# q and k in three tiles of 17, 17 and 16 chunks instead of five of 10, with eight output buffers and six held groups

## The chip, the cores and the metric

The kernel runs on one core of a Trainium2 chip. The core has a matrix engine (PE, with its weight loads shown as PEld), a vector engine (DVE), a scalar engine (ACT), a general engine (POOL), a queue engine (SP) and 16 DMA engines that move data between HBM and the on-chip memory. The metric is the time of one execution in microseconds; lower is better.

## The reference

Two stages. Per batch (B = 4, N = 6400 rows, C = 256 columns) an attention across channels, and then a mixture of eight low-rank adapters on every row of its result, of which each row takes two:

```python
qn = q / (norm(q, axis=1) + 1e-6);  kn = k / (norm(k, axis=1) + 1e-6)     # over the 6400 rows
s  = kn.T @ qn / tau                                                      # 256 x 256 per batch
a  = softmax(s, axis=-1)
x  = v @ a                                                                # 6400 x 256 per batch
logits = x @ w_gate                                                       # 8 experts
w  = softmax over the two largest logits of a row
out = x + sum over those two e of  w_e * (x @ A[e]) @ B[e]                # rank 16
```

So all of a batch's q and k must be read before the first output row of that batch can be made, while v is used row by row. Inputs and outputs are fp32 in HBM.

## The kernel before

**Chunks.** A batch's 6400 rows are 50 chunks of 128 rows; partition p holds rows 50p to 50p + 49, so a load of n chunks reads n KB in one piece per partition. Loads of q, k and v are issued on POOL and turn fp32 into bf16 on the way: a 10-chunk row becomes 5 KB. q and k share one tile (`qk`, both halves, `PC` = 10 chunks, `QKB` = 4 buffers). v comes in tiles of 18, 16 and 16 chunks (`VP`, three buffers); for batch 0 each of these is loaded in two pieces, all but 8 chunks and then 8. The v of the last batch (20, 20, 10 chunks) uses the q/k ring, which is free by then. One tile (`SPLIT`) is loaded in several row pieces.

**Per chunk.** `gram` (L265) adds k^T q of one chunk to a PSUM bank with two matmuls (L271). `square` (L253) squares q and k of two chunks at once on ACT (L261) or, for every second pair of batch 0, on DVE (L263); `norm` (L276) sums the squares on PE. After the 50th chunk, `chain0` to `chain6` make the softmax and fold it into two matrices: `a` for y and `wa` for logits and rank-16 products. `chain2` (L327) multiplies a scaled copy of the gram (`tk`) by a broadcast factor into `s_sb` (L331 to L334).

**Per pair of chunks** (100 pairs, called units u): four PE transposes of v (`transposes`, L421) with a copy to SBUF; after every five units a group is complete, its `logits` and `gating` follow (with one exponential on ACT, L490); then `z_gz` (L527), `gz_t`, `y_mm` (L543) and `delta` (L563), which copies the result into the group's output buffer on ACT (L567).

**Order.** All is written out by hand. First batch 0: squares, grams and norms of its 50 chunks. Then 100 slots: slot s transposes unit s, and carries the grams of the next batch that the table `GRAM` deals it (batch 1 in slots 0 to 20, batch 2 in 24 to 45, batch 3 in 49 to 67), while z and y of earlier units follow some groups behind. Squares of a slot stand at its start, so ACT and DVE meet them in that order.

**Loads.** A list sorted by the slot that needs each load is issued in order by `load_more` (L144): a load whose buffer is still in use stops all behind it. Each DMA on POOL also waits for the one issued eight places before it. Before the identity matrices are made on POOL, four q/k tiles of batch 0 are asked for (`load_more(3)`, `load_more(1)`); the first 4 chunks come by SP.

**Stores.** An output group is a 1.31 MB buffer, `YB` = 9 of them, the first of which serves as staging at the start. `send` (L577) issues stores on ACT's queue: it holds back `DEFER` = 7 complete groups while loads are left to issue, and one fewer for every three slots after the last load is issued. The last ten units are stored in small pieces on SP (L571).

Of the kernel before, what the change touches and what calls it, by code (L numbers as in the profile page):

```python
# [8 lines left out]
FP32 = mybir.dt.float32  # L9
BF16 = mybir.dt.bfloat16  # L10
AX = mybir.AxisListType
OP = mybir.AluOpType
ACT = mybir.ActivationFunctionType
# [3 lines left out]
def kernel(  # L17
# [16 lines left out]
    nc = tc.nc  # L34
    B, N, C = q.shape
    P = 128
    NC = N // P
    CC = C // P
# [3 lines left out]
    assert ER == P and CC == 2 and N % P == 0  # L42
    inv_tau = 1.0 / float(tau)

    PC = 10
    NPAIR = NC // 2
    NPT = B * NPAIR
    GRP = 5
    QKB, VB, YB = 4, 3, 9

    VP = [[18, 16, 16]] * 3 + [[20, 20, 10]]
    SPLIT = (1, 2)
    ROWS, ROWS_C = (7, 34, 6, 68, 13), 2
    FIRST = 4
    DEFER = 7

    GRAM = {1: (0, 20), 2: (24, 45), 3: (49, 67)}
    assert B == 4 and NC == 50
# [13 lines left out]
    one = ctx.enter_context(tc.tile_pool(name="one", bufs=1))  # L72
# [13 lines left out]
    qk_need = {}  # L86
    for b, (first, last) in GRAM.items():
        n = last - first + 1
        for c in range(NC):
            s = first + c * n // NC  # L90
            todo.setdefault(s, []).append((b, c))
            qk_need.setdefault((b, c // PC), s)


    loads = []

    for s in range(NC // PC):
        o = FIRST if s == 0 else 0
        loads.append((-10 + s, "qk", 0, s, o, [6, 4] if s == NC // PC - 1 else [PC - o]))
        for b in range(1, B):  # L100
            loads.append((qk_need[b, s], "qk", b, s, 0, [PC]))
    for b in range(B):
        for s, n in enumerate(VP[b]):
            at = NPAIR * b + sum(VP[b][:s]) // 2 + 1
            if b == 0:
# [6 lines left out]
    tiles = {"qk": {}, "v": {}}  # L112
    left = {"qk": [], "v": []}
# [4 lines left out]
    def ring(kind, b):  # L118
        return "qk" if b == B - 1 else kind

    def piece(kind, b, c):

        if kind == "qk":
            return divmod(c, PC)
        s = 0
        while c >= VP[b][s]:
            c -= VP[b][s]
            s += 1
# [5 lines left out]
    def load_by_rows(dst, src, m):  # L134

        dst = dst.rearrange("p (g c) d -> p g c d", g=2)
        src = src.rearrange("p (g c) d -> p g c d", g=2)
        nc.gpsimd.dma_start(dst[:, :, ROWS_C:m // 2, :], src[:, :, ROWS_C:m // 2, :])
        r = 0
        for n in ROWS:  # L140
            nc.gpsimd.dma_start(dst[r:r + n, :, 0:ROWS_C, :], src[r:r + n, :, 0:ROWS_C, :])
            r += n

    def load_more(limit=1000):  # L144

        while limit and at_load[0] < len(loads):
            _, kind, b, s, o, parts = loads[at_load[0]]
            if (kind, b, s) not in where:
                r = ring(kind, b)
                n = len(left[r])  # L150
                if n >= bufs[r] and left[r][n - bufs[r]]:
                    return
                where[kind, b, s] = n
                left[r].append(PC if kind == "qk" else VP[b][s])
                if r == "qk":
                    t = qk_pool.tile([P, 2, PC, C], BF16, tag="qk", name="qk")
                    if kind == "v":
                        t = t.rearrange("p w c d -> p (w c) d")
                else:
                    t = v_pool.tile([P, max(VP[b]), C], BF16, tag="v", name="vt")  # L160
                tiles[kind][b, s] = t
            t = tiles[kind][b, s]
            c0 = s * PC if kind == "qk" else sum(VP[b][:s])
            for m in parts:
                if kind == "qk":
                    nc.gpsimd.dma_start(t[:, 0, o:o + m, :], q_v[b, :, c0 + o:c0 + o + m, :])  # L166
                    nc.gpsimd.dma_start(t[:, 1, o:o + m, :], k_v[b, :, c0 + o:c0 + o + m, :])
                elif (b, s) == SPLIT:
                    load_by_rows(t[:, o:o + m, :], v_v[b, :, c0 + o:c0 + o + m, :], m)
                else:  # L170
                    nc.gpsimd.dma_start(t[:, o:o + m, :], v_v[b, :, c0 + o:c0 + o + m, :])
                o += m
            at_load[0] += 1
            limit -= 1
# [13 lines left out]
    DL = E * C // P  # L188
    nc.sync.dma_start(ast, moe_A.rearrange("e (h l) r -> (e h) (l r)", l=DL))
    load_more(3)  # L190
    ones_bf = const.tile([P, P], BF16)
    nc.vector.memset(ones_bf, 1.0)
# [4 lines left out]
    for c in range(0, FIRST, 2):  # L197
        t = tiles["qk"][0, 0]
        nc.vector.tensor_copy(t[:, 0, c:c + 2, :], stage[:, 0, c:c + 2, :])
        nc.scalar.copy(t[:, 1, c:c + 2, :], stage[:, 1, c:c + 2, :])  # L200
    load_more(1)
    ident = const.tile([P, P], BF16)
    make_identity(nc, ident)
    ident_f = const.tile([P, P], FP32)
    make_identity(nc, ident_f)
    load_more(3)

    wg_sb = const.tile([P, CC, E], BF16)
# [43 lines left out]

    def square(b, c, eng):  # L253

        s, o = divmod(c, PC)
        t = tiles["qk"][b, s]
        sq = sq_pool.tile([P, 2, 2, C], BF16, tag="sq", name="sq")
        sqs[b, c] = sq
        src = t[:, :, o:o + 2, :]
        if eng == "act":  # L260
            nc.scalar.activation(sq, src, ACT.Square)  # L261
        else:
            nc.vector.tensor_tensor(out=sq, in0=src, in1=src, op=OP.mult)  # L263

    def gram(b, c):  # L265
        if c == 0:
# [60 lines left out]
    def chain2(b):  # L327
        d = st[b]
        bc = nrm[b][:, 256:512]
        nc.tensor.matmul(bc, ones_f, d["dg"].rearrange("p c d -> p (c d)"), start=True, stop=True)  # L330
        s_sb = one.tile([P, CC, C], FP32, name="s_sb")  # L331
        for ic in range(CC):
            nc.vector.tensor_tensor(out=s_sb[:, ic, :], in0=bc, in1=d["tk"][:, ic, :], op=OP.mult)
        d["s"] = s_sb  # L334

    def chain3(b):
# [44 lines left out]
    def chain6(b):  # L381
        d = st[b]
        a_bf = bat.tile([P, CC, C], BF16, name="a_bf")
        for ic in range(CC):
# [3 lines left out]


    CHAIN = [(chain0, 0.0), (chain1, 0.9), (chain2, 0.75), (chain3, 0.0), (chain4, 0.55),  # L390
             (chain5, 0.65), (chain6, 0.5)]

# [184 lines left out]
    def send(keep):  # L577


        eng = nc.scalar  # L580
        while len(unsent) > keep:
            gr = unsent.pop(0)
            c0, n = 2 * (gr["f"] - gr["b"] * NPAIR), 2 * gr["n"]
            eng.dma_start(out_v[gr["b"], :, c0:c0 + n, :], gr["ys"][:, 0:n, :])
# [4 lines left out]
    for c in range(0, NC, 2):  # L589
        square(0, c, "act" if (c // 2) % 2 else "dve")  # L590
        gram(0, c)
        gram(0, c + 1)
        load_more()

        if c == 12:
            mask, sel = spread_masks()
        elif c in (20, 24, 28, 32):
            spread_rows(c - 20, 4)
        elif c == 36:
            cast_constants()  # L600
            spread()
        if c >= 4:
            norm(0, c - 4)
            norm(0, c - 3)
# [31 lines left out]
    while nz < NPT or zq is not None or dq is not None:  # L636
# [7 lines left out]
        for b, c in items:  # L644
            if c % 2 == 0:
                square(b, c, "act")
        if f in (chain0, chain1, chain2, chain3):
            f(fb)
# [15 lines left out]
        if at_load[0] < len(loads):  # L664
            all_loads[0] = slot
        send(max(0, DEFER - (slot - all_loads[0]) // 3))
        if behind:
# [53 lines left out]
```

## Time and profile before

| | |
|---|---|
| time, median of 3 runs (lowest, highest) | 255.47 us (255.2, 255.64) |
| the profiled execution's own time | 255.28 us |
| its span in the trace | 253.5 us |
| PE, DVE, ACT, POOL busy | 222.4, 155.5, 176.5, 35.4 us |
| granted PE clock, mean | 0.964 |
| HBM read, written | 78.91 MB, 26.21 MB: 415 GB/s over the span |

Times in the trace are counted from the span's start. A row of the timeline gives start, duration, engine, line, operation, output and input, and in brackets the idle time before it with what ended it; "q" behind an engine's name means its queue processor, which issues DMAs. In the chain a row is start, length and what held the end up. In a table by stretches a row gives a stretch, its length, the busy time of each engine with the number of instructions, the granted PE clock, the share of the DMA engines and GB/s. Rows of DMA issues give output and input, queue, count, KB each (as written) and the time from issue to landing.

### The profile page before, as it was taken

How to read it: one execution, taken by the hardware profiler on the slowest of the kernel's cores; microseconds unless marked ns; L12 is line 12 of the kernel's file. 1: busy time of each engine (PE TensorE's matmuls, PEld its weight loads, DVE VectorE, ACT ScalarE, POOL GpSimd, SP SyncE). 2: the span in 40 equal slices, each digit the busy share in tenths (PEclk: the TensorE clock that was granted, in tenths of full speed). 3: DMA queues.
4: the chain of work that ended last, by engine and by line, in shares of the span. 5: the costliest groups of instructions: out<-in, count | busy, mean ns of one | idle time of the engine just before them, and what ended most of it. 6: DMA issues, size and time to landing. Idle time of an engine off the chain costs nothing.

```text
span 253.5 us, 7433 instructions
## 1 busy us (share of the span) xinstructions
PE 222.4 (88%) x3122; PEld 191.8 (76%) x3122; DVE 155.5 (61%) x583; ACT 176.5 (70%) x291; POOL 35.4 (14%) x70
## 2 busy tenths in 40 slices
PE   0769793895999999999999989999998899999991
PEld 0436471684899978989999878989997689999980
DVE  1325534355477677785876867667588487777760
ACT  2434353867388788877888787888865967778881
POOL 8031221112111010512140202000000000000000
PEclk9988999598699999999999999999999999999999
DMA  7999999999999999999999999999999999999996
GB/s 211 230 213 217 208 218 212 213 218 213 213 212 215 220 210 216 219 211 214 201 216 215 211 253 278 221 309 267 271 267 282 294 363 427 426 422 424 423 413 274
DMA packets 13953, 66.81 MB, mean 264 GB/s; under 512 B 2528, under 2 KB 3040, under 8 KB 10720
## 3 DMA queue, kind: packets, MB, share of 16 engines
q0 software_dynamic: 9600, 38.80, 75.4%
q10 hardware_dynamic: 2592, 23.59, 22.4%
q1 hardware_dynamic: 1728, 3.94, 4.3%
q8 instruction: 24, 0.39, 0.6%
q14 instruction: 9, 0.07, 0.1%
HBM read 78.91 MB, written 26.21 MB: 415 GB/s over the span
## 4 chain that ended last, share of the span: by engine, by line
PE 56%; DMA 28%; DVE 8%; ACT 3%; issue 3%; POOL 1%; DVEq 0%; ACTq 0%; POOLq 0%
PE y_ps L543 14%; DMA qk<-in_k_dram 13%; DMA vt<-in_v_dram 9%; PE acc L271 9%; PE zg L527 7%; PE y_ps L563 7%; PE vT_ps L421 6%; DMA out_dram<-ys 6%; PE zg L551 4%; PE nrm L288 3%; PE vT_ps L442 3%; ACT sq L261 2%; DVE gz L531 2%; ACT ys L567 1%; DVE lm L477 1%
## 5 line engine op out<-in xcount | busy, mean ns | idle before, releaser
L261 ACT ACTIVATE sq<-qk 128x1024 bf16<-128x1024 bf16 x87 | 89.6, 1054 | 18.6 <-DMA qk<-in_k_dram 12.3
L271 PE MATMUL acc<-qk 128*128 128x256 bf16 x400 | 75.1, 289 | 13.8 <-DMA qk<-in_k_dram 7.3
L567 ACT COPY ys<-y_ps 128x512 f32<-128x512 f32 x100 | 58.7, 587 | 24.8 <-PE y_ps L563 20.4
L543 PE MATMUL y_ps<-a_bf,vT 128*128 128x256 bf16 x400 | 60.3, 273 | 1.5 <-ACT ys L567 1.5
L271 PEld LDWEIGHTS <-qk 128*128 128x128 bf16 x400 | 34.7, 102 | 24.0 <-DMA qk<-in_k_dram 9.3
L531 DVE TENSOR_TENSOR gz<-zg,gate 128x256 bf16<-128x256 f32 x100 | 41.6, 417 | 14.3 <-PE zg L527 12.8
L432 DVE COPY vT<-vT_ps 128x512 bf16<-128x512 bf16 x63 | 26.7, 423 | 28.0 <-PE vT_ps L421 27.3
L288 PEld LDWEIGHTS <-sq 128*128 128x128 bf16 x600 | 36.4, 98 | 7.0 <-ACT sq L261 2.8
L527 PE MATMUL zg<-wa_sb,vT 128*128 128x128 bf16 x400 | 38.7, 220 | 1.2 <-DVE gzT L557 1.0
L563 PE MATMUL y_ps<-ball_sb,gzT 128*128 128x256 bf16 x200 | 38.5, 274 | 0.0
L288 PE MATMUL nrm<-ones_bf,sq 128*128 128x1 bf16 x600 | 35.9, 165 | 1.2 <-ACT sq L261 1.2
L543 PEld LDWEIGHTS <-vT 128*128 128x128 bf16 x400 | 33.6, 97 | 4.4 <-issue 1.6
L421 PE MATMUL vT_ps<-ident,vt 128*128 128x128 bf16 x300 | 30.1, 225 | 1.4 <-DMA vt<-in_v_dram 1.1
L430 ACT COPY vT<-vT_ps 128x512 bf16<-128x512 bf16 x37 | 21.7, 586 | 10.6 <-PE vT_ps L421 9.2
L551 PE MATMUL zg<-ident,gz 128*128 128x128 bf16 x200 | 27.9, 221 | 1.1 <-DVE gz L531 0.6
L527 PEld LDWEIGHTS <-vT 128*128 128x128 bf16 x400 | 26.1, 97 | 3.3 <-issue 2.1
L421 PEld LDWEIGHTS <-vt 128*128 128x128 bf16 x300 | 22.7, 100 | 3.6 <-DMA vt<-in_v_dram 1.3
L557 DVE COPY gzT<-zg 128x256 bf16<-128x256 bf16 x90 | 25.2, 280 | 0.0
L166 POOL DMA_DIRECT2D qk<-in_q_dram x21 | 11.5, 549 | 77.5 <-ACT sq L261 23.0
L263 DVE TENSOR_TENSOR sq<-qk 128x1024 bf16<-128x1024 bf16 x13 | 9.1, 701 | 19.6 <-DMA qk<-in_k_dram 11.1
L551 PEld LDWEIGHTS <-gz 128*128 128x128 bf16 x200 | 15.3, 98 | 2.9 <-DVE gz L531 2.5
L563 PEld LDWEIGHTS <-gzT 128*128 128x128 bf16 x200 | 16.1, 98 | 0.4
(73 smaller groups left out, 202.3 us busy)
## 6 DMA issues: line engine op xcount, KB each, us to landing
out_dram<-ys ACTq DMA_DIRECT2D x18, 1280.0 KB, 17.3
qk<-in_q_dram POOLq DMA_DIRECT2D x18, 640.0 KB, 18.9
qk<-in_k_dram POOLq DMA_DIRECT2D x18, 640.0 KB, 22.4
vt<-in_v_dram POOLq DMA_DIRECT2D x3, 1024.0 KB, 28.2
vt<-in_v_dram POOLq DMA_DIRECT2D x5, 512.0 KB, 22.4
qk<-in_v_dram POOLq DMA_DIRECT2D x2, 1280.0 KB, 30.5
vt<-in_v_dram POOLq DMA_DIRECT2D x2, 1152.0 KB, 18.4
out_dram<-ys SPq DMA_DIRECT2D x3, 512.0 KB, 6.2
```

The lines of the kernel that those rows point to most:

```text
L261: nc.scalar.activation(sq, src, ACT.Square)
L271: nc.tensor.matmul(acc[b][:, ic, :], t[:, 1, o, ic * P:(ic + 1) * P], t[:, 0, o, :], start=(c == 0 and ic == 0), stop=(c == NC - 1), skip_ ...
L288: nc.tensor.matmul(nrm[b][:, j:j + 1], sq[:, w, c % 2, ic * P:(ic + 1) * P], ones_bf[:, 0:1], start=(c == 0 and j == 0), stop=(c == NC - 1 ...
L421: nc.tensor.matmul(pt[:, ic, sc * P:(sc + 1) * P], vt[:, o + sc, ic * P:(ic + 1) * P], ident, is_transpose=True, start=(i == 0), stop=(i = ...
L432: nc.vector.tensor_copy(dst, src)
L527: nc.tensor.matmul(z[:, sc, :], r["vT"][:, ic, sc, :], st[b]["wa"][:, ic, E:E + ER], start=(sc == 0 and ic == 0), stop=(sc == 1 and ic == ...
L531: nc.vector.tensor_tensor(out=gz.rearrange("p c (e r) -> p c e r", e=E), in0=z.rearrange("p c (e r) -> p c e r", e=E), in1=gr["gate"][:, r ...
L543: nc.tensor.matmul(y[:, sc, :], r["vT"][:, ic, sc, :], st[b]["a"][:, ic, :], start=(sc == 0 and ic == 0), stop=False, skip_group_check=True)
L551: nc.tensor.matmul(gt[:, sc, :], r["gz"][:, sc, :], ident, is_transpose=True, start=(sc == 0), stop=(sc == 1))
L557: nc.vector.tensor_copy(gzT, gt)
L563: nc.tensor.matmul(r["y"][:, sc, :], r["gzT"][:, sc, :], ball_sb, start=False, stop=(sc == 1), skip_group_check=True)
L567: nc.scalar.copy(gr["ys"][:, r["w"]:r["w"] + 2, :], r["y"])
```

## The change

q and k of a batch are cut into tiles of 17, 17 and 16 chunks (`QKP`) with three buffers, so 51 chunks of room in place of 40. Batch 0's tiles are loaded in pieces of 6 and 7 (behind the 4 from SP), 9 and 8, and 8, 4 and 4 chunks; other batches' tiles in one piece. A pair of chunks can now lie across two tiles (chunks 16 and 17), and is then squared in two instructions. The last batch's v is cut into 34 and 16 chunks. There are eight output buffers and six held groups. `chain2` writes its product over `tk` in place of a buffer of its own.

```diff
-    PC = 10
+    PC = 17
+    QKP = [17, 17, 16]
...
-    QKB, VB, YB = 4, 3, 9
+    QKB, VB, YB = 3, 3, 8
 
-    VP = [[18, 16, 16]] * 3 + [[20, 20, 10]]
+    VP = [[18, 16, 16]] * 3 + [[34, 16]]
...
-    DEFER = 7
+    DEFER = 6
...
-    for s in range(NC // PC):
+    for s, n in enumerate(QKP):
         o = FIRST if s == 0 else 0
-        loads.append((-10 + s, "qk", 0, s, o, [6, 4] if s == NC // PC - 1 else [PC - o]))
+        loads.append((-10 + s, "qk", 0, s, o, [[6, 7], [9, 8], [8, 4, 4]][s]))
         for b in range(1, B):
-            loads.append((qk_need[b, s], "qk", b, s, 0, [PC]))
+            loads.append((qk_need[b, s], "qk", b, s, 0, [n]))
...
-                left[r].append(PC if kind == "qk" else VP[b][s])
+                left[r].append(QKP[s] if kind == "qk" else VP[b][s])
...
     def square(b, c, eng):
...
+        if o < PC - 1:
+            parts = [(sq, tiles["qk"][b, s][:, :, o:o + 2, :])]
         else:
+            parts = [(sq[:, :, 0, :], tiles["qk"][b, s][:, :, o, :]),
+                     (sq[:, :, 1, :], tiles["qk"][b, s + 1][:, :, 0, :])]
+        for dst, src in parts:
+            if eng == "act":
+                nc.scalar.activation(dst, src, ACT.Square)
+            else:
+                nc.vector.tensor_tensor(out=dst, in0=src, in1=src, op=OP.mult)
...
-        s_sb = one.tile([P, CC, C], FP32, name="s_sb")
+        s_sb = d["tk"]
         for ic in range(CC):
-            nc.vector.tensor_tensor(out=s_sb[:, ic, :], in0=bc, in1=d["tk"][:, ic, :], op=OP.mult)
+            nc.vector.tensor_tensor(out=s_sb[:, ic, :], in0=bc, in1=s_sb[:, ic, :], op=OP.mult)
```

More of the change, by code (lines that the diff above doesn't have):

```diff
@@ L253, in square @@
     def square(b, c, eng):
-        s, o = divmod(c, PC)
-        t = tiles["qk"][b, s]
         sq = sq_pool.tile([P, 2, 2, C], BF16, tag="sq", name="sq")
         sqs[b, c] = sq
-        src = t[:, :, o:o + 2, :]
-        if eng == "act":
-            nc.scalar.activation(sq, src, ACT.Square)
-        else:
-            nc.vector.tensor_tensor(out=sq, in0=src, in1=src, op=OP.mult)
+        s, o = divmod(c, PC)
+        if o < PC - 1:
+            parts = [(sq, tiles["qk"][b, s][:, :, o:o + 2, :])]
+        else:
+            parts = [(sq[:, :, 0, :], tiles["qk"][b, s][:, :, o, :]),
[5 more added lines that the diff above has]
+                nc.vector.tensor_tensor(out=dst, in0=src, in1=src, op=OP.mult)
     def gram(b, c):
```

## The prediction

> **What bounds the kernel now.** I read the page first (slices, queues), then the chain, then the stretches around the places where the chain is a transfer.
>
> ```profile
> span 253.5 us, 7433 instructions
> ...
> PE   0769793895999999999999989999998899999991
> ...
> PEclk9988999598699999999999999999999999999999
> DMA  7999999999999999999999999999999999999996
> ...
> q0 software_dynamic: 9600, 38.80, 75.4%
> q10 hardware_dynamic: 2592, 23.59, 22.4%
> ```
>
> The DMA engines are full nearly all the time, and PE too from slice 10 on. The chain tells which of the two decides where:
>
> ```profile
> 16.80 19.07 DMA qk<-in_k_dram
> ...
> 39.21 23.02 DMA vt<-in_v_dram
> 62.28 0.61 PE vT_ps L421 x4
> ...
> 182.13 14.24 DMA out_dram<-ys
> 196.44 0.59 ACT ys L567
> ...
> 248.01 0.59 ACT ys L567
> ```
>
> Up to 62.3 us the arrival of data decides. Batch 0's last k piece lands at 35.87 and the third v piece at 62.23; slot 9's transposes start on it at 62.28. From there it is compute, with one more transfer, a store that lands at 196.4.
>
> ```profile
> core 0: us, PE busy (x) PEld busy (x) DVE busy (x) ACT busy (x) POOL busy (x), PEclk, DMA share, GB/s
> 57.50:60.00 2.50, 0.48 (x9) 0.29 (x6) 1.34 (x6) 0.79 (x2) 0.07 (x1) 1.00 1.04 210
> 63.00:66.00 3.00, 3.00 (x31) 2.44 (x30) 0.97 (x3) 0.78 (x1) 0.74 (x2) 0.50 1.05 215
> 66.00:69.00 3.00, 3.00 (x48) 2.69 (x47) 1.90 (x8) 1.54 (x2) 0.18 (x2) 0.62 1.02 206
> 73.00:77.00 4.00, 4.00 (x65) 3.74 (x63) 2.26 (x7) 3.06 (x5) 0.53 (x1) 1.00 1.05 213
> L421 PE MATMUL vT_ps<-ident,vt x56: 215/219/315, 47.2 to 73.2; 128*128 128x128 bf16 x56
> 73.08 0.39 PE L421 MATMUL vT_ps<-ident,vt 128*128 128x128 bf16 x4
> ```
>
> Around 73 to 77 us PE is busy 4.00 of 4.00 us at full clock: time lost ahead of that point has nothing to be won back from. The last two rows place slot 13: 56 transposes are 14 slots, and the fourteenth set starts at 73.08.
>
> **Order of the loads (the main term).** The rate: between 35.87 and 62.23 land 60 chunks of q and k of batch 1 and 26 of v, 86 chunks in 26.36 us, 0.3065 us each. In the changed program the loads after batch 0 stand as: 34 chunks (q and k, 0 to 16), v 10, v 8, 34 (17 to 33), v 8, 32 (34 to 49), v 8 (chunks 26 to 33), v 8, v 8. A q/k tile is now 34 chunks in front of the v piece behind it, where it was 20. Landings by that rate from 35.87, with the slot that needs them:
> - first v, 44 chunks: 49.4 (slot 0; it was 30 chunks, 45.1).
> - second q/k tile, 86 chunks: 62.2. Its first chunk, 17, is used in slot 7.
> - third v, 94: 64.7 (slot 9; was 62.2).
> - third q/k tile, 126: 74.5 (slot 14).
> - fourth v, 134: 76.9 (slot 13; was 114 chunks, 70.8).
>
> ```profile
> 47.20 0.63 PE L421 MATMUL vT_ps<-ident,vt 128*128 128x128 bf16 x4
> 56.23 0.38 PE L271 MATMUL acc<-qk 128*128 128x256 bf16 x2
> 48.39 0.53 POOL L171 DMA_DIRECT2D vt<-in_v_dram  x1 [2.51 <-DMA qk<-in_q_dram]
> vt<-in_v_dram POOLq DMA_DIRECT2D x1, 512.0 KB, 22.4
> ```
>
> The last two rows check the rate: that v piece was issued at 48.39 and took 22.4, so 70.8. It was no wait then, since slot 13 came at 73.08. It becomes one: slot 13 cannot start before 77.0, 3.9 us late. The other way to the same place: slot 7's first gram (56.23 now) waits for 62.2, and the six slots from there took 73.08 - 56.23 = 16.9 us, 2.0 of them idle (the stretch from 57.50 above, 0.48 busy of 2.50), so 62.2 + 14.9 = 77.1. Both give 77. Behind the same wait stands ACT: the square of chunks 16 and 17 is issued in slot 6, its second half waits for chunk 17, and behind it in ACT's queue are the first group's exponential (so its gates) and the squares from 18 on. They have until 77 and need eight squares of 1.05 us, so they cost nothing beside PE's own wait. From slot 13 on I keep +3.9; later tiles land 2 to 10 us ahead of their slots by the same count, so nothing gives it back or adds.
>
> **Start.** All 14 loads of batch 0 now stand ahead of the identity matrices on POOL, and each waits for the one eight places before it. The last waits for the sixth, 52 of batch 0's 100 chunks (8 of them by SP): 35.87 - 48 x 0.3065 = 21.2, so the matrices come at 21 to 23 in place of 5.67:
>
> ```profile
> 5.67 0.24 POOL masks.py:197 MEMSET ident<- 128x128 bf16 x1
> 21.73 0.60 PE L271 MATMUL acc<-qk 128*128 128x256 bf16 x4
> 22.65 0.61 PE L271 MATMUL acc<-qk 128*128 128x256 bf16 x4
> ```
>
> DVE's masks at chunk 12 wait for them, behind them its squares, behind those PE's norms: PE stands at about 24.5 where data were there at 21.2. Bounds 0 to +2 at the end of batch 0; when data are there PE takes 0.92 us per two chunks (22.65 - 21.73) against 4 x 0.3065 = 1.23 of transfer and has 14 us to catch up, so I take 0. The cover is slot 0's wait for v until 49.4, 2.2 us after 47.20, and then slot 7's.
>
> **Stores.** Eight output buffers and six held groups: group 12's first copy now needs group 4's store landed, where it needed group 3's; either is issued after 55 copies. So the distance is the same and what counts is how long the store takes beside the loads.
>
> ```profile
> out_dram<-ys ACTq DMA_DIRECT2D x1, 1280.0 KB, 10.9
> out_dram<-ys ACTq DMA_DIRECT2D x1, 1280.0 KB, 14.2
> 182.13 0.34 ACTq L584 DMA_DIRECT2D out_dram<-ys  x1
> 196.44 0.58 ACT L567 COPY ys<-y_ps 128x512 f32<-128x512 f32 x1 [2.87 <-DMA out_dram<-ys]
> 155.20 0.56 POOL L171 DMA_DIRECT2D vt<-in_v_dram  x1
> DMA to landing us min/median/max: 29.6/29.6/29.6
> ```
>
> From the queues' shares: q0's 75.4% of 16 x 253.5 us over 38.80 MB is 0.079 us per KB written, q10's 22.4% over 23.59 MB 0.0385. A store's row (10 KB) takes 0.39 us, a load's row of 10 chunks (5 KB) 0.40, of 20 chunks 0.81, of 34 chunks (17 KB) 1.37. The first store (146.6, beside 10-chunk rows) took 10.9 us, that of 182.13 (beside 20-chunk rows) 14.2. With 8 rows per engine, taken in turn with load rows: 10.9 = a + 8 x 0.79 gives a = 4.6, and 4.6 + 8 x 1.20 = 14.2, as measured. So a load's long row holds the store up.
> In the changed kernel the 34-chunk load of v starts when the v piece before it is in, 184.8 now (155.20 + 29.6), plus most of one more store sent by then (1.31 MB, 3.1 us): about 187. It needs 34 x 0.3065 = 10.4 us alone and 13.4 in turn with store rows, to 200. Group 4's store goes out at 182.13 + 3.9 = 186.0, its rows from about 189.5: six beside 34-chunk rows (6 x 1.76), two beside 16-chunk ones (2 x 1.03), and 1.1 at the end: it lands near 203. The copy is ready at 196.44 - 2.87 + 3.9 = 197.5 and waits 5.5 us, 2.6 more than now. Bounds: -2.9 (no wait) to +5.5 (all eight rows beside 34-chunk ones and both wait and load later). I take +2.6, by the row of 182.13, the nearest.
>
> **The rest.**
> ```profile
> L261 ACT ACTIVATE sq<-qk 128x1024 bf16<-128x1024 bf16 x87 | 89.6, 1054 | 18.6 <-DMA qk<-in_k_dram 12.3
> L430 ACT COPY vT<-vT_ps 128x512 bf16<-128x512 bf16 x37 | 21.7, 586 | 10.6 <-PE vT_ps L421 9.2
> out_dram<-ys SPq DMA_DIRECT2D x2, 256.0 KB, 3.9
> stage<-in_q_dram SPq DMA_DIRECT2D x1, 512.0 KB, 3.9
> ```
> Squares: one per batch is halved; a half on ACT lies between 0.53 and 1.05, by the 128x512 copy 0.59, so 2 x 0.59 - 1.05 = +0.1 each; +0.2 for those beside a full PE. The product in place in chain2 has the same 8 instructions, its buffer's last reader is a batch earlier: 0. PE's sequence is unchanged. End: the last stores took 3.9 us behind others; a 512 KB load with nothing ahead also took 3.9, of which half its bytes are 0.6, so with compute later and the queue empty 3.3: -0.6.
> Sum, on the profiled execution's 255.28 (0.19 below the median 255.47): 255.28 + 3.9 + 2.6 + 0.2 - 0.6 = 261.4.
>
> **Rivals.**
> Transfers set the end, faster: 11 of POOL's 62 DMAs go. From the v pieces' landings,
> ```profile
> 57.04 0.53 POOL L171 DMA_DIRECT2D vt<-in_v_dram  x1 [1.96 <-DMA qk<-in_q_dram]
> 60.06 0.53 POOL L171 DMA_DIRECT2D vt<-in_v_dram  x1 [2.50 <-DMA qk<-in_k_dram]
> vt<-in_v_dram POOLq DMA_DIRECT2D x1, 512.0 KB, 21.8
> ```
> the second lands 81.9 - 79.4 (22.4 for the first too) = 2.4 us after the first for 8 chunks, 0.303 each, no more than in 10-chunk loads: a fixed cost per DMA is at most about 0.2 us, 11 x 0.2 = 2.2, 253.1. It decides only if the fourth v lands by 73.0, 134 chunks in 37.1 us, 10% faster than any row. The Trainium skill ("DMA: Bandwidth & Descriptors", Anatomy of one DMA) fits about 2.0 us fixed per DMA beside the bytes; paid one after another that would be 22 us, 233; the spacing just shown disagrees, since the transfers overlap.
> The store's wait stays as it is (loads' rows are cut shorter, or the large load is over earlier): 258.8. It vanishes: 255.9, about no change.
> The clock: PE idles before 60 and runs at 0.50 to 0.62 until 69. A longer idle stretch at slot 7 (58.5 to 62.2) that costs one more 3.4 us stretch at half clock takes 1.7 us more: 263.1. The Trainium skill ("TensorE: Matmul & The Clock Gate", Part 1) has half rate after an idle window of about 3.4 us and full rate after a busy one; by it the wait at slot 13, under 1 us, costs no clock, and the rows agree so far.
> The store waits for all of the 34-chunk load: 264.3.
>
> **Numbers.** Sum as forecast 0.50 (260 to 263); wait unchanged 0.17; wait gone 0.06; clock 0.12; whole load 0.06; faster 0.09. Range 257 to 265. About 0.2% is what can be told from no change: faster 0.09, same 0.04, slower 0.87.
>
> **What would show it.** Right: PE idle 58 to 62 on the k load, slot 13's transposes on the v load near 77, ACT's copy waiting some 5 us on a store near 198 to 203, the tail moved by 6. Wrong: slot 13 before 75, or the store landing within 12 us.

## The result, and the profile after

The changed kernel takes 259.75 us (median of 5, 258.95 to 260.76) against 255.45 us before: a ratio of 1.0174, 95% interval 1.0157 to 1.0191. It is slower by 4.3 us, where 261.4 was forecast, in the range of 257 to 265. The execution that was profiled took 260.49 us, span 258.7, so the trace has to explain 5.2 us of span.

The page of the changed kernel, the lines that answer to those of before:

```profile
span 258.7 us, 7416 instructions
...
PE   0768793794999999999999989999999589999993
...
PEclk9997999577799999999999999999999899999999
DMA  7999999999999999999999999999999999998495
...
q0 software_dynamic: 8016, 38.80, 73.0%
q10 hardware_dynamic: 2592, 23.59, 22.0%
```

The same bytes move in fewer packets. Two things are new (slices counted from 0): the DMA engines, full up to the last slice before, fall to 8 and 4 in slices 36 and 37, so the transfers now wait for compute near the end; and PE has a hole in slice 31, with a lower clock just behind it. The chain (start, length, what held the end up) names two transfers after 46 us:

```profile
46.39 30.24 DMA vt<-in_v_dram
76.68 0.40 PE vT_ps L427 x4
...
185.76 16.61 DMA out_dram<-ys
202.44 0.59 ACT ys L573
...
255.01 0.58 ACT ys L573
```

The first is the fourth v piece, for slot 13 (73.08 before). The second is a store, on which the first copy of group 12 waits (196.44 before). The last copy starts at 255.01 (248.01 before). PE's and ACT's rows at those places, with the idle time and its end in brackets:

```profile
62.01 0.60 PE L277 MATMUL acc<-qk 128*128 128x256 bf16 x2 [3.63 <-DMA qk<-in_k_dram]
76.68 0.40 PE L427 MATMUL vT_ps<-ident,vt 128*128 128x128 bf16 x4 [0.64 <-DMA vt<-in_v_dram]
177.63 0.59 ACT L573 COPY ys<-y_ps 128x512 f32<-128x512 f32 x1 [1.37 <-DMA out_dram<-ys]
189.97 0.59 ACT L573 COPY ys<-y_ps 128x512 f32<-128x512 f32 x1 [2.29 <-DMA out_dram<-ys]
202.44 0.58 ACT L573 COPY ys<-y_ps 128x512 f32<-128x512 f32 x1 [4.40 <-DMA out_dram<-ys]
```

PE's idle time ahead of slot 13 stands mostly at slot 7, on the second q and k tile (3.63 us), and only 0.64 us of it at slot 13 itself, on the v piece.

ACT waits for stores three times, 8.1 us in all, where it waited once, 2.87 us. These are the first copies of groups 10, 11 and 12. While the store of 185.76 is out, PE runs dry, and then runs at a lower clock (stretches: engines' busy time, clock, DMA share, GB/s):

```profile
194.00:199.00 5.00, 5.00 (x78) 4.56 (x76) 3.82 (x16) 3.36 (x7) 0.00 (x0) 1.00 0.95 265
199.00:203.00 4.00, 0.85 (x11) 0.54 (x9) 1.96 (x9) 0.56 (x2) 0.00 (x0) 1.00 1.00 278
203.00:206.00 3.00, 2.90 (x26) 2.28 (x26) 1.08 (x5) 2.56 (x9) 0.00 (x0) 0.76 1.01 301
206.00:209.00 3.00, 2.77 (x31) 2.31 (x30) 1.41 (x7) 1.87 (x4) 0.00 (x0) 0.67 1.01 418
```

The end of PE's idle stretch there:

```profile
203.08 0.60 PE L549 MATMUL y_ps<-a_bf,vT 128*128 128x256 bf16 x4 [2.99 <-ACT ys L573]
```

What passes the DMA engines between 187 and 200 us, by queue (packets, MB, share of 16 engines):

```profile
q0 software_dynamic: 150, 2.06, 74.2%
q10 hardware_dynamic: 131, 1.31, 24.6%
```

In these 13 us 131 packets of stores have 24.6% of the engines, and the load, in about as many packets (150, among them 17 KB rows), 74.2%. It is plainer between 179 and 183 us, where a store meets load rows of 16 chunks (8 KB) all the time:

```profile
q0 software_dynamic: 64, 0.53, 62.5%
q10 hardware_dynamic: 64, 0.66, 39.8%
```

That is 64 rows against 64, whatever their bytes: each side gets a turn per row, not a share of bytes or time.

Along the trace compute is late by 3.6 us at slot 13 (76.68 against 73.08), by 6.0 at the first copy of group 12, by 7.0 at the last copy (in fact from the fifth copy of group 12 on), and the end by 5.2, since the last store lands 2.0 us after its issue where it took 3.9 in the full queue.

### The profile page after: what moved, and what is told of

It is laid out like the page before. It is cut to its first block, busy times and chain, and to the rows that moved or that the text cites. A ratio compares the mean times of both kernels' runs of the same rounds, so it can differ in the third digit from the quotient of the medians.

```text
span 258.7 us, 7416 instructions
## 1 busy us (share of the span) xinstructions
PE 224.7 (87%) x3122; PEld 193.1 (75%) x3122; DVE 155.3 (60%) x584; ACT 176.6 (68%) x294; POOL 29.5 (11%) x59
## 4 chain that ended last, share of the span: by engine, by line
PE 51%; DMA 34%; DVE 7%; ACT 3%; issue 2%; POOL 1%; DVEq 0%; ACTq 0%; POOLq 0%
DMA qk<-in_k_dram 16%; PE y_ps L549 14%; DMA vt<-in_v_dram 12%; PE acc L277 8%; DMA out_dram<-ys 6%; PE zg L533 6%; PE y_ps L569 6%; PE vT_ps L427 6%; PE zg L557 4%; PE vT_ps L448 3%; PE nrm L294 3%; ACT sq L267 2%; DVE gz L537 2%; ACT ys L573 1%; DVE lm L483 1%
## 5 line engine op out<-in xcount | busy, mean ns | idle before, releaser
L267 ACT ACTIVATE sq<-qk 128x1024 bf16<-128x1024 bf16 (+1 forms) x90 | 90.2, 1026 | 24.7 <-DMA qk<-in_k_dram 18.4
L277 PE MATMUL acc<-qk 128*128 128x256 bf16 x400 | 76.5, 292 | 15.9 <-DMA qk<-in_k_dram 9.6
L427 PE MATMUL vT_ps<-ident,vt 128*128 128x128 bf16 x300 | 30.7, 228 | 1.8 <-DMA vt<-in_v_dram 1.8
L269 DVE TENSOR_TENSOR sq<-qk 128x1024 bf16<-128x1024 bf16 (+1 forms) x14 | 9.0, 652 | 13.9 <-DMA qk<-in_k_dram 7.2
L288 PE MATMUL nrm<-sq,ones_bf 128*128 128x512 bf16 x50 | 16.4, 420 | 0.0
```

Source lines behind the costliest of these rows:

```text
L267: nc.scalar.activation(dst, src, ACT.Square)
L277: nc.tensor.matmul(acc[b][:, ic, :], t[:, 1, o, ic * P:(ic + 1) * P], t[:, 0, o, :], start=(c == 0 and ic == 0), stop=(c == NC - 1), skip_ ...
L427: nc.tensor.matmul(pt[:, ic, sc * P:(sc + 1) * P], vt[:, o + sc, ic * P:(ic + 1) * P], ident, is_transpose=True, start=(i == 0), stop=(i = ...
```

## The experiments

The theory: two losses add up in compute, the late q and k tile and v piece (3.6 us at slot 13) and the store that takes turns with long load rows (2 to 3 us more waiting). Rivals: the eight buffers and six held groups make the store wait; the start (late identity matrices, halved squares) makes compute late; one limit alone decides. Eleven kernels ran; "the changed kernel" is that of the diff above. Each ratio is to the kernel before, timed beside the kernel in question; its median there was 255.29 us beside the first four kernels below, and 255.49 to 255.50 beside the others.

### Load rows of 17 and of 9 chunks

The 34-chunk load is issued as two or as four loads into the same buffer; nothing else differs.

```diff
-                loads.append((at, "v", b, s, 0, [n]))
+                loads.append((at, "v", b, s, 0, [17, 17] if n == 34 else [n]))
```
```diff
+                loads.append((at, "v", b, s, 0, [9, 9, 8, 8] if n == 34 else [n]))
```

> The changed kernel, with the 34-chunk v load issued as two of 17 into the same buffer; nothing else differs. Theory (a store's row waits for one load row each time): group 4's store takes 4.6 + 8 x (0.39 + 0.69) = 13.2 us in place of 16.6, lands near 199, group 12's first copy waits about 1 us in place of 4.4, and PE keeps its clock: total 255.5 to 257. Rival (fewer buffers and held groups are what makes the wait, or bytes are shared evenly whatever the row): 259.5 to 260.

> The changed kernel, with the 34-chunk v load issued as four of 9, 9, 8 and 8 into the same buffer. Theory (row length): the store takes 4.6 + 8 x (0.39 + 0.36) = 10.6 us, lands near 196.5 before the copy is ready at 198, no wait there; total 255 to 256, since only 1 us or so more is to be had before the stores at the end are limited by the transfers. Rival (buffers and held groups): 259.5 to 260.

Measured: 255.57 us (ratio to before 1.0013, 1.0003 to 1.0023) and 255.30 us (1.0002, 0.9992 to 1.0011). The store issued behind 55 copies, in rows of DMA issues (KB, us to landing), for rows of 34, 17 and 9 chunks in this order:

```profile
out_dram<-ys ACTq DMA_DIRECT2D x1, 1280.0 KB, 16.6
```
```profile
out_dram<-ys ACTq DMA_DIRECT2D x1, 1280.0 KB, 13.6
```
```profile
out_dram<-ys ACTq DMA_DIRECT2D x1, 1280.0 KB, 10.8
```

13.2 and 10.6 were expected for the last two. ACT's waits for stores (us in total, times, longest) sum to 8.1 in the changed kernel and 4.2 with rows of 17; with rows of 9 there is none:

```profile
ACT ys L573 <- DMA out_dram<-ys: 8.1, 3, 4.4
```
```profile
ACT ys L573 <- DMA out_dram<-ys: 4.2, 2, 2.2
```

Both kernels have eight buffers and six held groups, so these alone do not make the wait in this order of loads. Cutting one load's rows takes back what the change cost (all but 0.3 us with rows of 17, all with rows of 9), although slot 13 is as late as in the changed kernel (76.8 and 76.6). The changed kernel with nine buffers was not run, so it is open whether one more buffer would have hidden the 17 KB rows as well.

### Batch 1's q and k in two pieces

```diff
-            loads.append((qk_need[b, s], "qk", b, s, 0, [n]))
+            if b == 1:
+                h = (n + 1) // 2
+                loads.append((qk_need[b, s], "qk", b, s, 0, [h]))
+                loads.append((0.5 + (s * PC + h) * 21 // 50, "qk", b, s, h, [n - h]))
+            else:
+                loads.append((qk_need[b, s], "qk", b, s, 0, [n]))
```

> The changed kernel, with batch 1's q and k tiles loaded in two pieces each (9 and 8 chunks, 8 and 8), the second piece at its own place in the list. Theory (order of the loads): the fourth v piece is behind 118 chunks in place of 134, so it lands near 72 us in place of 76.6, slot 13 starts at 73 to 73.6 (76.68 in the changed kernel, 73.08 before). The store wait then takes part of it back, since the 34-chunk load of v still runs from about 187 to 200: group 12's first copy is ready at about 194.8 and waits some 6 us, to 200 to 201 (202.44 now). Total 257.5 to 258.5 (changed kernel 259.75). Rival (the 3.6 us come from the start, that is from the late identity matrices or the halved squares): slot 13 stays at 76 to 77, total 259.7.

Measured: 262.18 us (1.0259, 1.0228 to 1.0291), worse than the changed kernel; a miss. Its first half came true: slot 13 starts at 72.2 (73 to 73.6 expected), so the order of the loads did make compute late there, and not the start. But the next batch's v piece lands at 97.7 as it did (97.5), so slot 25 is only 1.65 us earlier than in the changed kernel. And at slot 61 PE meets batch 3's last q and k tile:

```profile
181.10 0.39 PE L282 MATMUL acc<-qk 128*128 128x256 bf16 x2 [3.40 <-DMA qk<-in_k_dram]
```

Compute that is earlier also issues its stores earlier (163.0 and 172.9 in place of 164.9 and 174.7); they take their turns ahead of that tile, which lands at 181.05 in place of 178.97. What was won by 1.8 us is lost by 3.4, and then comes the store behind 34-chunk rows again (4.3 us) with the clock at 0.50 from 204 to 210.

### Both edits

> The changed kernel with both edits: batch 1's q and k in two pieces, the 34-chunk v load in four. Theory: slot 13 at 73 to 73.6, no wait of 4 us for a store; compute ends some 7 to 8 us earlier than in the changed kernel, but the transfers, full from 2 us on, then set the end as they did before: 254 to 255.5. Rival (something else of the change costs the time): above 257.

Measured: 256.0 us (1.0041, 1.0021 to 1.0060), 0.7 more than with the short rows alone, above the expected 255.5 by half a microsecond. Slot 13 is at 72.2, and the last copy at 250.5 (249.4 with the short rows alone). The same tile holds compute up again: ACT's square waits 2.10 us for it at 180.3. Being early in batch 1 is worth nothing here.

### Buffers and held groups, in the kernel before

```diff
-    QKB, VB, YB = 4, 3, 9
+    QKB, VB, YB = 4, 3, 8
-    DEFER = 7
+    DEFER = 6
```

> The kernel before, with eight output buffers and six held groups and nothing else changed. Theory (the store wait depends on the rows of the loads beside it): the distance between a store and the copy that needs its buffer is the same, the first copy of group 12 waits some 3 us as before; total 255 to 256.5. Rival (the buffers make the wait): 257 to 259.

and with the nine buffers kept:

> The kernel before, with six held groups in place of seven and its nine buffers kept. Theory: one more store goes ahead of the second v piece of batch 2, which lands near 173 in place of 168.6 and holds slot 59 up by some 3 us, as in the run with eight buffers; but group 12's first copy needs a store issued five copies sooner, so no wait for it: total 255.3 to 256.5. Rival (the wait for v alone makes the 3.3 us of the run with eight buffers): 258 to 259.

Measured: 258.8 us (1.0126, 1.0106 to 1.0145), a miss, and 256.14 us (1.0029, 1.0016 to 1.0041), as expected. In both the second v piece of batch 2 comes late to slot 59 (at 173.2 and 173.4, 168.6 before; PE's rows of the two kernels):

```profile
173.25 0.61 PE L421 MATMUL vT_ps<-ident,vt 128*128 128x128 bf16 x4 [4.16 <-DMA vt<-in_v_dram]
```
```profile
173.48 0.40 PE L421 MATMUL vT_ps<-ident,vt 128*128 128x128 bf16 x4 [3.96 <-DMA vt<-in_v_dram]
```

A group fewer held means one store more ahead of that load. The first expectation counted only the store's own wait. With nine buffers that wait is gone (0 in place of 3.9 us) and the 4 us for v are nearly covered; with eight they add up. In the changed kernel this v piece stands ahead of the last q and k tile and lands at 165.7, so there the cost shows elsewhere, if at all. In the kernel before, then, the buffers and held groups do cost 3.3 us by themselves; the result with short rows says only that they cost nothing beside the changed kernel's loads.

### Five held groups in the changed kernel

```diff
-    DEFER = 6
+    DEFER = 5
```

> The changed kernel with five held groups in place of six, so every store is issued five copies sooner. Theory: the wait of group 12's first copy goes (its buffer's store is issued 10 us earlier), but one more store stands before batch 3's last q and k tile, which lands 3 us later, near 182, where slot 61 needs it at 179: a wait of about 3 us there; total 256.5 to 259. Rival (holding groups back is what costs): below 256.

Measured: 261.11 us (1.0224, 1.0208 to 1.0239), above the expected 256.5 to 259; a miss. ACT waits for no store any more, and PE waits where expected (3.64 us). Behind that wait the clock is 0.50 from 183 to 189 us, which the expectation left out: slot 62 comes at 186.3 in place of 180.8.

```profile
183.77 0.61 PE L277 MATMUL acc<-qk 128*128 128x256 bf16 x2 [3.64 <-DMA qk<-in_k_dram]
183.00:189.00 6.00, 5.23 (x47) 4.36 (x48) 2.35 (x9) 4.12 (x6) 0.00 (x0) 0.50 1.08 269
```

### The late v piece alone, in the kernel before

```diff
-                loads.append((at + (n - 8) // 2, "v", b, s, n - 8, [8]))
+                loads.append((at + (n - 8) // 2 + (3 if s == 1 else 0), "v", b, s, n - 8, [8]))
```

> The kernel before, with only the fourth v piece of batch 0 moved behind batch 1's last q and k tile: 134 chunks behind batch 0 in place of 114. Theory (time lost there is not won back): it lands at 76.9, slot 13 starts near 77 in place of 73.08, compute stays 3.9 us late up to the store wait, whose 2.87 us may change by 1 either way; total 258 to 259.7. Rival (compute has slack behind it): 255 to 256.5.

Measured: 258.44 us (1.0118, 1.0102 to 1.0133), as expected. PE waits for the piece, and nothing is won back by the last copy, 4.3 us late at 252.3:

```profile
76.74 0.50 PE L421 MATMUL vT_ps<-ident,vt 128*128 128x128 bf16 x3 [4.12 <-DMA vt<-in_v_dram]
```

### No store wait, with and without the late piece

In the kernel before, the 20-chunk loads of the last v are issued as two of 10:

```diff
-                loads.append((at, "v", b, s, 0, [n]))
+                loads.append((at, "v", b, s, 0, [10, 10] if n == 20 else [n]))
```

> The kernel before, with the two 20-chunk loads of the last v issued as two of 10 each. Theory (row length): the store of group 3 takes 10.9 us in place of 14.2, the wait of 2.87 us goes. Compute ends nearly 3 us earlier, but the stores at the end then stand in the full DMA queue, so the time falls by less: 254 to 255.2. Rival (row length does not matter): 255.4, and the wait stays 2.9.

> The kernel before, with the last v in loads of 10 chunks and the fourth v piece moved behind batch 1's last q and k tile. Theory (two limits, the later one counts): slot 13 starts near 77 as in the run with the late piece alone, there is no store wait to add to it, the last copy comes at 249 to 250 in place of 245.5, still in time for stores that the transfers hold until 252.5; total 255.3 to 256 where the late piece alone took 258.4. Rival (a late piece always costs its 3 to 4 us): 258 to 259.5.

Measured: 255.56 us (1.0003, 0.9994 to 1.0013), above the expected 254 to 255.2, and 257.24 us (1.0067, 1.0053 to 1.0080). The first has no store wait (the store takes 11.1 us) and its last copy is 2.5 us earlier, at 245.5, but its last store lands at 252.6 as in the kernel before (252.5). The second lies between the two theories: its last copy is at 251.4, 5.8 us later, and its end only 1.7 us later. So there is a floor, and the late piece is partly free. The expectation counted 3.9 us of delay; slot 13 was also earlier without the late piece (71.4), so it was 5.5.

### The row-wise load issued whole

```diff
-    SPLIT = (1, 2)
+    SPLIT = None
```

> The kernel before, with the last v in loads of 10 chunks and the row-wise load of one v tile issued whole. Theory (transfers set the end, and the stretch with the row pieces moves 197 to 201 GB/s where its neighbours move 212): 0.3 to 0.5 us less than with the row pieces, 254.9 to 255.3. Rival (the row pieces cost nothing, or they keep the DMA engines level): 255.5 or more.

Measured: 256.09 us (1.0023, 1.0013 to 1.0033), slower than with the row pieces (255.56): the rival came true. GB/s in the 40 slices of the page, of this kernel and then of the one with row pieces:

```profile
GB/s 210 230 214 216 208 218 213 213 215 212 217 212 214 222 209 217 214 214 216 216 218 212 211 261 270 228 307 269 259 304 320 315 329 389 427 424 422 423 416 211
```
```profile
GB/s 211 226 219 212 210 215 216 211 218 214 212 213 214 219 211 218 219 208 219 198 214 217 213 284 246 242 290 273 256 306 316 319 319 368 428 421 421 426 421 274
```

The stretch of the row pieces (198, now 216) is faster without them, but the last slice moves 211 in place of 274. Why the end drains more slowly is open; that the pieces keep the 16 engines level was not measured engine by engine.

### All runs side by side

Places in time (us) are of one profiled execution each, the last column is the median of the timed runs. Medians of kernels timed apart differ by up to 0.2 us for the same kernel, so the ratios above decide and not this column; and the profiled execution of the kernel before with 8 buffers and 6 held took 261.18 us, 2.4 more than its median, and that of the changed kernel with rows of 17 took 256.48, 0.9 more, so their places lie later than a run at the median would have them.

| kernel | slot 13 | first copy of group 12 | last copy | last store landed | median us |
|---|---|---|---|---|---|
| before | 73.1 | 196.4 | 248.0 | 252.5 | 255.45 |
| changed | 76.7 | 202.4 | 255.0 | 257.7 | 259.75 |
| rows of 17 | 76.8 | 200.1 | 251.0 | 253.7 | 255.57 |
| rows of 9 | 76.6 | 197.2 | 249.4 | 252.4 | 255.30 |
| batch 1 in pieces | 72.2 | 203.6 | 257.1 | 259.7 | 262.18 |
| both | 72.2 | 198.3 | 250.5 | 253.2 | 256.0 |
| changed, 5 held | 77.1 | 204.0 | 256.2 | 258.9 | 261.11 |
| before, 8 buffers, 6 held | 71.3 | 202.8 | 255.5 | 258.4 | 258.8 |
| before, 6 held | 72.0 | 197.9 | 250.4 | 253.4 | 256.14 |
| before, late v | 76.7 | 200.8 | 252.3 | 255.3 | 258.44 |
| before, rows of 10 | 71.4 | 193.0 | 245.5 | 252.6 | 255.56 |
| the same, late v | 76.9 | 198.9 | 251.4 | 254.3 | 257.24 |
| rows of 10, v tile whole | 73.0 | 193.4 | 246.0 | 253.2 | 256.09 |

Where the last copy starts after about 249.5, the last store lands 2.6 to 3.0 us behind it; where it starts earlier, the store lands at 252.4 to 253.2 all the same. The kernel before, with its copy at 248.0, had some 1.7 us of room to that floor. No version ran faster than the kernel before.

## Why the prediction was right, and where it was off

**Order of the loads.** The rate held for every piece: first v at 49.17 (49.4 forecast), the second q and k tile 61.96 (62.2), third v 64.41 (64.7), third tile 74.22 (74.5), fourth v 76.64 (76.9). Slot 13 came at 76.68, 3.6 us late where 3.9 was said. The piece-wise load moved slot 13 back to 72.2, and the late piece alone gave 76.74 in the kernel before, so the cause is shown. Both ways to 77 that the prediction counted were there: the wait at slot 7 took 3.63 us, and the v piece only 0.64 us on top, so without that last wait slot 13 would have come near 76.0 all the same (an estimate from these rows; no run moves one of the two alone in the changed kernel). That compute wins nothing back is shown too (+3.6 at slot 13 as at slots 50 and 60). What failed here is the sentence that later tiles land 2 to 10 us ahead of their slots: batch 3's last q and k tile landed at 178.97, and its first use in PE came at 179.4:

```profile
179.36 0.38 PE L277 MATMUL acc<-qk 128*128 128x256 bf16 x2
```

The changed kernel got past it with 0.4 us to spare, and the runs that moved stores or compute forward ran into it.

**Start.** The identity matrices came at 20.82 (21 to 23 forecast, so a little earlier) and cost nothing that shows: slot 0 waited for v until 49.2 as said.

**Stores.** The load row of 17 KB was reckoned at 1.37 us and the store's landing at 203; it landed at 202.4, 16.6 us after its issue (17 forecast). The rows of 17 and 9 chunks showed the form to hold at two more points, so this mechanism is shown. The wait itself came out otherwise: 4.40 us and not 5.5, since the copy was ready at 198.0 (197.5 forecast) and the store landed at 202.4 (203). Two earlier stores, beside rows of 16 chunks and at the end of 34, already held ACT for 1.37 and 2.29 us, which the forecast had left at no wait. Copy by copy, the first of these is made good (3.6 us late again at the fourth copy of group 10), and the second leaves 0.9 (4.5 late at the last copy of group 11). With 1.5 us more waiting for the third store (4.40 in place of 2.87) that makes the 2.4. So the term of 2.6 was met nearly, but by two waits where it had one. The delay at that copy is 6.0 against a forecast 6.5.

**The clock.** I gave a lower clock a case of its own at slot 7; it did not come there beyond what the kernel before had, but at the store wait: 0.76 and 0.67 in the stretches from 203, which makes 3.4 us at half clock, and compute went from 6.0 to 7.0 us late just there. The sum had nothing for it. The Trainium skill ("TensorE: Matmul & The Clock Gate", Part 1) has half rate after an idle window of about 3.4 us. The trace agrees in direction, but not in the length of the idle stretch: here the clock fell behind 2.99 us, and in the kernel with batch 1 in pieces the clock stayed at 1.00 from 181 to 184 behind an idle stretch of 3.40 us. So in these runs the length of a wait near 3 us does not tell whether the clock falls.

**The end.** The term of -0.6 was mis-sized: the last copy was 7.0 us late and the end 5.2, so it was -1.8. I had taken the store's landing from a load of the start with nothing ahead (3.3 us); the last one landed in 2.0. This is the floor of the table seen from the other side: before, compute had about 1.7 us of room, and only delay beyond that counts.

**The sum**, on the profiled execution: 3.6 + 2.4 (6.0 less 3.6) + 1.0 (clock) - 1.8 = 5.2, forecast 6.1; the halved squares' 0.2 cannot be told apart. That the forecast came so near is in part luck: the clock's 1.0, which it left out, and the end, where it took 1.2 too little off, nearly cancel. The remaining 0.7 us of the miss lie in the runs: the median is 259.75 where the profiled one took 260.49.

**The rivals.** That transfers set the end in spite of all was said to need the fourth v by 73.0. This was too narrow: with the rows of 9 chunks the piece is late by 3.5 us and the time is that of the kernel before, since the store waits are gone. What the rival said of its gain is refuted: eight DMAs fewer on POOL bring nothing to the floor (the last store lands at 252.4 with 17-chunk tiles and rows of 9, 54 DMAs, and at 252.5 in the kernel before, 62 DMAs).

## What to carry to other kernels

Where loads and stores share the DMA engines row by row, the length of a load's rows sets how long a store takes, and so when its buffer comes free; cut the rows of the loads that run beside stores, not the bytes. When a list of loads is cut more coarsely, count for each piece what lands ahead of it and compare that with the slot that needs it: here 20 chunks more in front of one v piece (134 in place of 114) made it land 5.8 us later, and 3.6 of them reached compute. And when two limits lie within 2 us of each other, price each delay by the later of the two ends, not by its own size.

## What the runs showed of the hardware

A store of 1.31 MB took 16.6, 13.6 and 10.8 us beside load rows of 17, 8.5 and 4 to 4.5 KB, and from 179 to 183 us the DMA engines moved 64 store rows of 10 KB and 64 load rows of 8 KB: turns by row. The Trainium skill ("DMA: Bandwidth & Descriptors", Queues, rings and completion order) says that an engine takes the rows of queues in turn and drains a whole packet before it switches; the trace agrees if one row of up to 17 KB counts as a packet. Issuing one tile whole instead of by uneven row pieces, which looked like a gain in its own stretch, cost 0.5 us at the end of the kernel, and why is open. An idle stretch of PE of 2.99 us was followed by 3.4 us at half clock, and one of 3.40 us was not.
